# The first FFN product of the last two row groups as seven block products over eight PSUM banks

## The chip, the core and the metric

The kernel runs on one core of one Trainium2 chip. The metric is the device time of one execution in microseconds (us); the time before is 584.73 us, the median of three runs (584.64 to 585.35). The engines are named as in the profile: PE (TensorE, with PEld for its weight loads), DVE (VectorE), ACT (ScalarE), POOL (GpSimd) and SP (SyncE, which issues DMAs).

## What is computed

Attention with a squared ReLU, then a block of Fourier mixing, normalization and a feed-forward network (FFN):

```python
scores = (1 / sqrt(64)) * q @ k.T                      # 8 batches, 12 heads, 448 rows, 64 columns
x = (maximum(scores, 0) ** 2 / 448) @ v                # heads side by side: 8 x 448 x 768
u = x + real(fft(fft(x, axis=1), axis=2))
un = (u - mean(u)) / sqrt(var(u) + 1e-6)               # over the 768 columns
out = u + maximum(un @ w_ch1, 0) @ w_ch2               # w_ch1 768 x 3072, w_ch2 3072 x 768
```

The change touches `maximum(un @ w_ch1, 0)` for the last 512 of the 3584 rows.

## The kernel before

**Stages.** Batch after batch goes through attention (scores on PE, ReLU on ACT, square on DVE or ACT, product with v on PE), the mixing by DFT matrices, and the normalization; the normalized rows go to DRAM and come back transposed. The FFN runs over groups of rows: one of 384, one of 512, one of 384 and nine of 256 (`GT`, line 194; groups 0 to 11). Its matmuls fill PE between the parts of attention; after the last attention product only FFN groups are left.

**What sets the order.** All instructions are issued in an order that a planner in the kernel makes at build time (`Streams`, line 63). Every piece of work is a generator that asks with `need(engine, duration, deps, buffers)`; the planner takes the request that can start first by its own cost figures (`mm`, `act`, `dve`, line 141 on, and `LATENCY`, line 60). On the chip each engine runs its instructions in that order and waits on semaphores.

**PSUM.** There are eight banks: three tiles of two banks (`BS`, line 220, tags S0 to S2) and two single banks (`BF`, line 221). The FFN uses `BF`, attention and mixing mostly `BS`.

**A group's first product** (`ffn`, line 1383). `w1_sb[m][hf]` holds w_ch1 as six row blocks m of 128 and two column halves hf. For a group of 256 rows, `unT` holds the transposed rows as six blocks of 128x256. For each of 24 column blocks j, six matmuls (line 1452) sum up in half a bank; two blocks j share a bank, and `relu` (line 1409) moves 128x512 out to `h`, on ACT (line 1426) or DVE (line 1424). `unT` has two homes for the groups of 256 rows (`pair_homes`, line 1158), so the transposes of a group (line 1160) wait until the group two before has done its first product.

**A group's second product** (`Pair`, line 1536) is already done by seven block products (Strassen's scheme in Winograd's form), in two chains. Each product is 12 matmuls of 128x384 (line 1583). `chain_a` (line 1610) puts four products into one bank and `chain_b` (line 1631) one into one bank and two into another; after each, DVE adds the bank to an output tile `o` (line 1438), and the next product of that bank waits for this add (`t`). `early` and `late` (lines 1551 and 1572) form sums of blocks of `h` on DVE. The sums T of w_ch2 are made once (`weight_sums`, line 1281).

**Output tiles.** `outputs` (line 1353) has one stream for each of six slots: it loads a tile of u into `o` (line 1370), waits for the last add, stores it (line 1374), and waits for the store before it loads the next. Each group of 256 rows has four such tiles.

Of the kernel before, what the change touches and what calls it, by code (L numbers as in the profile page):

```python
# [9 lines left out]
FP32 = mybir.dt.float32  # L10
# [154 lines left out]
def kernel(  # L165
# [488 lines left out]
        BX[m].free.append(e)  # L654
        x_ready[b][m].t = e

    chains = [0]

    def attention(b, left=None):

# [8 lines left out]
        while pa < NB:  # L669
# [38 lines left out]
            for part in ("scores", "values") if few else ("values", "scores"):  # L708
                if part == "values" and values:
                    held = homes.take()  # L710
                    av = held[:, 0] if homes is BS else held
                    give = lambda when, homes=homes, held=held: homes.give(held, when)
                    vn, h0 = loads[bv * NG + mv // 2][2], 2 * mv % HG
                    for c in range(4):
                        sq, _, at = sv.pop(4 * mv + c)
                        sq_ids.append((e, at))
                        for h in range(2):
                            nc.tensor.matmul(av[h * Dh:(h + 1) * Dh, 0:S], lhsT=vn[:, c, h0 + h, :],  # L718
                                             rhs=sq[:, h, :], start=(c == 0), stop=(c == 3))
                        BSQ.free.append(e)  # L720
                    av_end = e - (n * mm(S) + SWITCH if n and not few else 0.0) + LATENCY["PE"]
                    if mv % 2 == 1:
                        BQ[2].free.append(e)
                    if left is None:
# [651 lines left out]
            yield need("SP", 0.0, [e])  # L1376

    def ffns():
        for b in range(NGR):
            yield need("SP", 0.0, [group_ready[b]])  # L1380
            yield from ffn(b)

    def ffn(b):
        T0, N, unT = groups[b]
# [24 lines left out]
        def relu(ph, e, j):  # L1409
# [18 lines left out]
            for x in ht[j:j + JN]:  # L1428
                x.t = e + LATENCY["ACT"]

        left = {(c, hf): 1 + (b > 0 and hf == 1 if c in WHOLES[b] else (c % 2, hf) != (0, 1))
                for c in range(NC) for hf in range(2)}

        def add(pc, e, c, hf, give=True):

            e = yield need("DVE", dve(DH), [e + LATENCY["PE"], ot[b, c, hf]])
            o = os[b, c, hf]
            nc.vector.tensor_tensor(o, pc[:, 0:DH], o, op=ALU.add)  # L1438
            if give:
                BF.give(pc, e)  # L1440
            left[c, hf] -= 1
            if not left[c, hf]:
                added[b, c, hf].t = e + LATENCY["DVE"]
            return e + LATENCY["DVE"]

        for j in range(0, JC, JN):
            hf, jj = divmod(j, JC // 2)
            e = yield need("PE", 6 * JN * mm(N), [w1_ready[hf]] + ([group_ready[b]] if b > 1 else []), [BF])
            ph = BF.take()
            for i in range(JN):  # L1450
                for m in range(MC):
                    nc.tensor.matmul(ph[:, i * N:(i + 1) * N], lhsT=w1_sb[m][hf][:, (jj + i) * 128:(jj + i + 1) * 128],  # L1452
                                     rhs=unT[:, m, 0:N], start=(m == 0), stop=(m == MC - 1))
            advance(6 * JN * mm(N))
            sch.add(relu(ph, e, j), (0, 0))
            if j == JC // 2:
                ffn_begun[b].t = e
                pairs = [Pair(b, c, h, ht, add, advance) for c in PAIRS[b]]
                for p in pairs:
                    sch.add(p.early(), (0, 0.3))  # L1460
                    sch.add(p.late(), (0, 0.3))
        if b == 0:
            unt_left.t = e
        else:
            BUNT.free.extend([e, e] if b == 2 else [e])

        for c in WHOLES[b]:
            if b > 0:
# [67 lines left out]
    class Pair:  # L1536
# [1 line left out]

        read = []

        def __init__(self, b, c, h, ht, add, advance):
            self.b, self.c, self.h, self.ht, self.add, self.advance = b, c, h, ht, add, advance
            self.L, self.R = slice(c * 128, c * 128 + 128), slice(c * 128 + 128, c * 128 + 256)
            self.ev = [slice(2 * i0, 2 * i1, 2) for i0, i1 in CH]
            self.od = [slice(2 * i0 + 1, 2 * i1, 2) for i0, i1 in CH]
            self.r12, self.r4 = ([Cell() for _ in CH] for _ in range(2))
            self.m1, self.m2, self.done = Cell(), Cell(), [Cell(), Cell()]
            self.reads = Cell(), Cell()
            self.waits, Pair.read = Pair.read, [self.reads[0], self.reads[1], *self.r4]

        def early(self):

            h, L, R_ = self.h, self.L, self.R
            if not made:
                yield need("DVE", 0.0, [un_left])
                a1 = work.tile([128, 6, 128], BF16, name="s1", tag="un2", bufs=1)
                a2 = work.tile([128, 6, 128], BF16, name="s2", tag="un3", bufs=1)
                at = JC * 256 + KP * DH
                for a, m in ((a1, upper(at, 6, 128)), (a2, upper(at + 6 * 128, 6, 128))):
                    made.append([a, m[:, 0:4], m[:, 4:6]])  # L1560
            for k, (i0, i1) in enumerate(CH):
                ev, od, s1, s2 = self.ev[k], self.od[k], made[0][k], made[1][k]
                d = dve2((i1 - i0) * 128)
                yield need("DVE", d, self.ht[2 * i0:2 * i1] + self.waits + ([upper_free] if k else []))
                nc.vector.tensor_tensor(s1, h[:, ev, R_], h[:, od, R_], op=ALU.add)
                yield need("DVE", d)
                nc.vector.tensor_tensor(s2, s1, h[:, ev, L], op=ALU.subtract)
                e = yield need("DVE", d)
                nc.vector.tensor_tensor(h[:, ev, R_], h[:, ev, L], h[:, ev, R_], op=ALU.subtract)
                self.r12[k].t = e + LATENCY["DVE"]  # L1570

        def late(self):

            h, L = self.h, self.L
            for k, (i0, i1) in enumerate(CH):
                e = yield need("DVE", dve2((i1 - i0) * 128), [self.m2, self.r12[k]])
                nc.vector.tensor_tensor(h[:, self.od[k], L], h[:, self.od[k], L], made[1][k], op=ALU.subtract)
                self.r4[k].t = e + LATENCY["DVE"]

        def product(self, pc, lhs, rhs, start, i0=0, i1=KP):  # L1580

# [5 lines left out]
        def first(self, k):  # L1587

            cut = KP - 3
            yield need("PE", cut * mm(DH), self.ht[k:2 * cut:2] + [self.m1] * k, [BF])  # L1590
            pc = BF.take()
            chains[0] += 1
            self.product(pc, self.block(k, self.L), self.weights(k, 0), True, 0, cut)
            e = yield need("PE", (KP - cut) * mm(DH), self.ht[2 * cut + k::2])
            self.product(pc, self.block(k, self.L), self.weights(k, 0), True, cut)
            return pc, e

        def block(self, k, cols):

            return [self.h[:, 2 * i + k, cols] for i in range(KP)]  # L1600

        def formed(self, n):

            return [made[n][k][:, i - i0] for k, (i0, i1) in enumerate(CH) for i in range(i0, i1)]

        def weights(self, k, hf):

# [23 lines left out]
        def chain_b(self):  # L1631
# [5 lines left out]
            e = yield need("PE", d, [sums[3]] + self.r12, [BF])  # L1637
            pc = BF.take()
# [27 lines left out]
    with tc.manual_schedule():  # L1666
# [11 lines left out]
        sch.add(attentions(), (3, 3))  # L1678
        sch.add(warming(), (9, 9))
        sch.add(weight_sums(), (6, 6))  # L1680
        sch.add(halve(), (3, 3))
        sch.add(turns(), (1, 1))
        for slot in range(6):
# [33 lines left out]
```

## Time and profile before

| | us |
|---|---|
| median of three runs | 584.73 |
| the profiled execution | 584.67 |
| its span, first to last instruction | 582.8 |
| PE busy in the span | 572.9 |
| DVE busy | 406.4 |
| ACT busy | 335.0 |
| POOL busy | 133.7 |

Busy time is summed over all stages. The view of windows gives it for a stretch of the span, with the granted PE clock (1.00 is full). A row of the chain of work names when a step began, how long it lasted, and its engine, tile, line and count. A row of groups ends with the busy time, the mean in ns, and the idle time before the group with what ended it. In the timeline a row gives start and length of a run of like instructions; in square brackets stands the idle time before it and its releaser.

### The profile page before, as it was taken

How to read it: one execution, taken by the hardware profiler on the slowest of the kernel's cores; microseconds unless marked ns; L12 is line 12 of the kernel's file. 1: busy time of each engine (PE TensorE's matmuls, PEld its weight loads, DVE VectorE, ACT ScalarE, POOL GpSimd, SP SyncE). 2: the span in 40 equal slices, each digit the busy share in tenths (PEclk: the TensorE clock that was granted, in tenths of full speed). 3: DMA queues.
4: the chain of work that ended last, by engine and by line, in shares of the span. 5: the costliest groups of instructions: out<-in, count | busy, mean ns of one | idle time of the engine just before them, and what ended most of it. 6: DMA issues, size and time to landing. Idle time of an engine off the chain costs nothing.

```text
span 582.8 us, 11457 instructions
## 1 busy us (share of the span) xinstructions
PE 572.9 (98%) x4476; PEld 365.7 (63%) x4476; DVE 406.4 (70%) x927; ACT 335.0 (57%) x511; POOL 133.7 (23%) x188
## 2 busy tenths in 40 slices
PE   8999999999999999999999999999999999999997
PEld 7566556544455546556857667568577786868684
DVE  5978667986669988787787878987946852222222
ACT  5866873587745787676668748777654340304040
POOL 8534021411115313421333032303300230000000
PEclk9998999999999999999999999999999999999999
DMA  9999999776947997699579987993433353031201
GB/s 120 206 211 227 222 210 134 173 131 95 181 57 189 207 172 168 116 216 167 122 123 207 180 153 147 200 176 115 126 75 100 118 151 99 30 94 36 79 30 55
DMA packets 133493, 81.85 MB, mean 140 GB/s; under 512 B 77504, under 2 KB 128704, under 8 KB 133440
## 3 DMA queue, kind: packets, MB, share of 16 engines
q0 software_dynamic: 40320, 33.63, 38.2%
q1 hardware_dynamic: 93120, 47.50, 36.3%
q8 instruction: 35, 0.57, 0.4%
q14 instruction: 18, 0.15, 0.1%
HBM read 62.91 MB, written 26.25 MB: 153 GB/s over the span
## 4 chain that ended last, share of the span: by engine, by line
PE 88%; DVE 6%; ACT 4%; issue 1%; POOL 0%; DVEq 0%; ACTq 0%; POOLq 0%
PE psF L1452 37%; PE psF L1583 26%; PE psS L736 6%; PE psF L718 5%; PE psF L1503 3%; PE psF L1477 3%; PE psS L1212 2%; ACT sq L761 2%; DVE sq L776 2%; PE psS L718 1%; PE psS L823 1%; PE psS L1026 1%; PE psS L1187 1%; PE psF L505 0%; ACT un L1087 0%
## 5 line engine op out<-in xcount | busy, mean ns | idle before, releaser
L1452 PE MATMUL psF<-unT,w 128*128 128x256 bf16 (+2 forms) x1728 | 229.8, 291 | 1.2 <-ACT unT L999 0.9
L1452 PEld LDWEIGHTS <-w 128*128 128x128 bf16 x1728 | 165.9, 98 | 61.6 <-issue 11.5
L761 ACT ACTIVATE sq<-psS 112x896 bf16<-112x896 f32 x192 | 164.4, 918 | 38.4 <-PE psS L736 38.0
L1426 ACT ACTIVATE hT<-psF 128x512 bf16<-128x512 f32 (+3 forms) x169 | 87.9, 532 | 116.6 <-PE psF L1452 115.8
L776 DVE TENSOR_TENSOR sq<-sq 112x896 bf16<-112x896 bf16 x161 | 100.6, 638 | 16.6 <-ACT sq L761 15.6
L1583 PEld LDWEIGHTS <-hT 128*128 128x128 bf16 x792 | 76.0, 98 | 54.4 <-issue 5.8
L1438 DVE TENSOR_TENSOR o<-psF,o 128x384 f32<-128x384 f32 x92 | 50.9, 553 | 44.8 <-PE psF L1583 39.6
L1583 PE MATMUL psF<-w,hT 128*128 128x384 bf16 x462 | 81.7, 326 | 0.3 <-DVE hT L1424 0.2
L736 PE MATMUL psS<-qkT 64*128 64x448 bf16 (+1 forms) x384 | 51.6, 359 | 1.2 <-ACT qkT L510 0.4
L718 PE MATMUL psF<-sq,vn 112*64 112x448 bf16 x320 | 37.9, 358 | 0.3 <-DVE o L1438 0.3
L557 DVE TENSOR_SCALAR xT<-psF 128x224 bf16<-128x224 f32 x58 | 19.8, 383 | 26.3 <-PE psF L718 26.2
L376 POOL DMA_DIRECT2D vn<-in_v_dram x24 | 17.3, 720 | 76.0 <-PE psS L736 67.7
L1059 POOL TENSOR_TENSOR u<-tp,xn 112x385 f32<-112x385 f32 (+2 forms) x14 | 13.3, 953 | 93.1 <-DVE tp L1041 81.5
L1583 PE MATMUL psF<-wsum,hT 128*128 128x384 bf16 x198 | 34.6, 326 | 0.0
L736 PEld LDWEIGHTS <-qkT 64*128 64x128 bf16 (+1 forms) x384 | 15.9, 102 | 28.7 <-issue 21.2
L376 POOL DMA_DIRECT2D qn<-in_q_dram x21 | 15.5, 739 | 69.9 <-DVE qkr L469 49.6
L718 PEld LDWEIGHTS <-vn 112*64 112x64 bf16 x384 | 17.8, 109 | 21.4 <-issue 13.7
L773 ACT ACTIVATE sq<-sq 112x896 bf16<-112x896 bf16 x31 | 29.5, 956 | 0.5
L1068 DVE BATCH_NORM_STATS2 stats<-u 112x6 f32<-112x384 f32 (+2 forms) x56 | 28.4, 541 | 0.0
L1087 ACT ACTIVATE un<-u,nmr,rstd 112x768 bf16<-112x768 f32 (+2 forms) x22 | 22.4, 1025 | 7.3 <-DVE nmr L1074 5.0
L1477 PE MATMUL psF<-w,hT 128*128 128x384 bf16 x144 | 25.1, 326 | 0.0
L1503 PE MATMUL psF<-w,hT 128*128 128x384 bf16 x144 | 24.7, 326 | 0.0
(166 smaller groups left out, 612.6 us busy)
## 6 DMA issues: line engine op xcount, KB each, us to landing
out_dram<-o SPq DMA_DIRECT2D x56, 192.0 KB, 2.2
vn<-in_v_dram POOLq DMA_DIRECT2D x24, 224.0 KB, 5.9
qn<-in_q_dram POOLq DMA_DIRECT2D x21, 224.0 KB, 5.3
kn<-in_k_dram POOLq DMA_DIRECT2D x21, 224.0 KB, 5.5
w<-in_moe_w_ch_dram POOLq DMA_DIRECT2D x12, 384.0 KB, 14.5
w<-in_moe_w_ch_dram POOLq DMA_DIRECT2D x4, 1152.0 KB, 20.5
utop<-u SPq DMA_DIRECT2D x12, 336.0 KB, 3.1
o<-utop SPq DMA_DIRECT2D x16, 192.0 KB, 3.8
```

What stands on the lines that cost most here:

```text
L376: nc.gpsimd.dma_start(out=t, in_=src[b, hs].rearrange("h (p j) d -> p h (j d)", j=4))
L718: nc.tensor.matmul(av[h * Dh:(h + 1) * Dh, 0:S], lhsT=vn[:, c, h0 + h, :], rhs=sq[:, h, :], start=(c == 0), stop=(c == 3))
L736: nc.tensor.matmul(sc[:wide, h, 0:S].rearrange("k (c q) -> k c q", c=4), lhsT=flat[ps, k0:k0 + wide], rhs=qT[ps, m % 2], start=True, stop= ...
L761: nc.scalar.activation(r, sc[:R, :, 0:S], AF.Relu)
L773: nc.scalar.activation(r, r, AF.Square)
L776: nc.vector.tensor_tensor(r, r, r, op=ALU.mult)
L1426: nc.scalar.activation(hs, ps, AF.Relu)
L1438: nc.vector.tensor_tensor(o, pc[:, 0:DH], o, op=ALU.add)
L1452: nc.tensor.matmul(ph[:, i * N:(i + 1) * N], lhsT=w1_sb[m][hf][:, (jj + i) * 128:(jj + i + 1) * 128], rhs=unT[:, m, 0:N], start=(m == 0), ...
L1477: nc.tensor.matmul(pc[:, 0:DH], lhsT=block(j, c), rhs=w2(j, hf), start=(j == 0), stop=(j == JC - 1))
L1503: nc.tensor.matmul(pc[:, 0:DH], lhsT=block(2 * i + k, c), rhs=weights[i], start=(start and i == 0), stop=(i == KP - 1), skip_group_check=True)
L1583: nc.tensor.matmul(pc[:, 0:DH], lhsT=lhs[i], rhs=rhs[i], start=(start and i == 0), stop=(i == KP - 1), skip_group_check=True)
```

## The change

Groups 10 and 11 get their first product together, in `last_two`, once both are transposed. With w_ch1 cut by halves of its rows (lo: m = 0 to 2, hi: m = 3 to 5) and by even and odd column blocks j, and with b1, b2 the transposed rows of groups 10 and 11, a 2x2 by 2x2 block product arises. `quarter_sums` forms on DVE the weight sums S1 = odd lo + odd hi, S2 = S1 - even lo, S3 = even lo - odd lo (in the place of odd lo), S4 = even hi - S2, 24 instructions of 128x768, and T1 = b2 lo - b1 lo, T2 = b2 hi - T1, T3 = b2 hi - b2 lo, T4 = b1 hi - T2, four more. For each pair of column blocks i = 0 to 11 there are seven products of three matmuls of 128x256:

- bank p (`main`): **M** = even lo x b1 lo; then **U2** adds S2 x T2, **U1** adds S1 x T1, **V** adds S4 x b2 hi. After M, U2 and U1 ACT copies the bank into SBUF; after V ACT applies the ReLU: that is the even block of group 11.
- bank r (`second`): **M'** = even hi x b1 hi. DVE adds the copy of M, then clamps at zero: the even block of group 10.
- bank q (`third`): **Q** = S3 x T3; DVE adds the copy of U1 and clamps: the odd block of group 11. Then **Q'** adds odd hi x T4; DVE adds the copy of U2 and clamps: the odd block of group 10.

U2, U1 and V wait for the copy before them; Q' waits for DVE's reading of q. The banks come from `B8`: the three two-bank tiles of `BS` as six banks, and the two of `BF`. Four sets of three copy tiles (`BK`) are in use in turn. `SLACK` (0.4) is added to what the planner assumes from a product to a copy and from a copy to a product. The ReLU results of group 10 lie where `h` lay, those of group 11 in tiles taken from attention.

The second products of both groups (`Pair`) are unchanged in their arithmetic; they take banks from `B8`, group 11's sums lie in four of the S tiles, and its `early` and `late` go in five pieces (of at most six column blocks) that don't cross its tiles. All four chains are in the planner's hands at once.

```diff
     def ffns():
-        for b in range(NGR):
+        for b in range(NGR - 2):
             yield need("SP", 0.0, [group_ready[b]])
             yield from ffn(b)
+        yield from last_two()
...
+    def quarter_sums():
+
+        yield need("SP", 0.0, [last_values])
...
+                yield from form(1, m, hf, w1_part(1, m, hf), w1_part(1, m + 3, hf), ALU.add)
+                yield from form(2, m, hf, S_[1][m, hf], w1_part(0, m, hf), ALU.subtract)
+                yield from form(4, m, hf, w1_part(0, m + 3, hf), S_[2][m, hf], ALU.subtract)
...
+                yield from form(3, m, hf, w1_part(0, m, hf), w1_part(1, m, hf), ALU.subtract, [ffn1_left],
+                                w1_part(1, m, hf))
...
+            e = yield need("DVE", dve2(768), [group_ready[ga], group_ready[gb]])
+            Tk[n] = homes[n - 1]
+            nc.vector.tensor_tensor(Tk[n], x(), y(), op=ALU.subtract)
...
+        B8 = Banks(6, lambda i: tiles[i // 2][:, i % 2] if i < 6 else plain[i - 6])
...
+        def product(ps, n, k, i, rhs, start, stop):
+
+            hf, ii = divmod(i, 6)
+            for m in range(3):
+                lhs = w1_part(n, m + k, hf)[:, ii] if k is not None else S_[n][m, hf][:, ii]
+                nc.tensor.matmul(ps[:, 0:N], lhsT=lhs, rhs=rhs[:, m], start=(start and m == 0),
+                                 stop=(stop and m == 2), skip_group_check=True)
+
+        d, half_done, SLACK = 3 * mm(N), Cell(), 0.4
+
+        late = LATENCY["PE"] + SLACK
+
+        def copy(ps, dst, e):
+            e = yield need("ACT", act(N), [e + late])
+            nc.scalar.copy(dst, ps[:, 0:N])
+            return e + LATENCY["ACT"] + SLACK
+
+        def sum_out(q, u, t, dst, deps, done, hta):
+            e = yield need("DVE", dve(N), deps, [BH[t]] if hta is not None else [])
+            nc.vector.tensor_tensor(dst, q[:, 0:N], u, op=ALU.add)
+            done(e)
+            e = yield need("DVE", 0.2)
+            nc.vector.tensor_scalar(dst, dst, 0.0, None, op0=ALU.max)
+            return e + LATENCY["DVE"] + SLACK
+
+        def main(i):
+
+            m1, u4 = Cell(), Cell()
+            e = yield need("PE", d, [], [B8, BK])
+            p, bk = B8.take(), BK.take()
+            cs = bk.aps
+            product(p, 0, 0, i, b1[:, 0:3], True, False)
+            sch.add(second(i, m1, cs), (5 + 0.1 * i, 5 + 0.1 * i))
+            m1.t = e = yield from copy(p, cs[0], e)
+            e = yield need("PE", d, [e, QS[2], QT[2]])
+            product(p, 2, None, i, Tk[2], False, False)
+            e = yield from copy(p, cs[1], e)
+            e = yield need("PE", d, [e, QS[1], QT[1]])
+            product(p, 1, None, i, Tk[1], False, False)
...
+            u4.t = e = yield from copy(p, cs[2], e)
+            e = yield need("PE", d, [e, QS[4]])
+            product(p, 4, None, i, b2[:, 3:6], False, True)
+            e = yield need("ACT", act(N), [e + late])
+            nc.scalar.activation(at_b(0, i, i + 1, every)[:, 0], p[:, 0:N], AF.Relu)
+            B8.give(p, e)
...
+        for n, p in enumerate(pairs):
+            sch.add(p.early(), (0, 7 + n))
+            sch.add(p.late(), (0, 7 + n))
+            sch.add(p.chain_a(), (7 + 1 * n, 0))
+            sch.add(p.chain_b(), (6.9 + 1 * n, 0))
+        yield need("SP", 0.0, pairs[1].done)
```

More of the change, by code (lines that the diff above doesn't have):

```diff
@@ L1378, in ffns, with adder, add @@
     def ffns():
-        for b in range(NGR):
+        for b in range(NGR - 2):
             yield need("SP", 0.0, [group_ready[b]])
             yield from ffn(b)
+        yield from last_two()
+    def adder(b, NC, pool):
+        left = {(c, hf): 1 + (b > 0 and hf == 1 if c in WHOLES[b] else (c % 2, hf) != (0, 1))
+                for c in range(NC) for hf in range(2)}
+        def add(pc, e, c, hf, give=True):
+            e = yield need("DVE", dve(DH), [e + LATENCY["PE"], ot[b, c, hf]])
+            o = os[b, c, hf]
+            nc.vector.tensor_tensor(o, pc[:, 0:DH], o, op=ALU.add)
+            if give:
+                pool.give(pc, e)
+            left[c, hf] -= 1
+            if not left[c, hf]:
+                added[b, c, hf].t = e + LATENCY["DVE"]
+            return e + LATENCY["DVE"]
+        return add
@@ L1429, in relu @@
                 x.t = e + LATENCY["ACT"]
[L1431 to L1444, printed above, removed]
+        add = adder(b, NC, BF)
         for j in range(0, JC, JN):
@@ L1457, in ffn @@
                 ffn_begun[b].t = e
-                pairs = [Pair(b, c, h, ht, add, advance) for c in PAIRS[b]]
+                at = lambda k, i0, i1, cols: h[:, 2 * i0 + k:2 * i1:2, cols]
+                pairs = [Pair(b, c, at, ht, add, advance, [(k, *ch) for k, ch in enumerate(CH)], BF) for c in PAIRS[b]]
                 for p in pairs:
@@ L1568, in early @@
                 e = yield need("DVE", d)
-                nc.vector.tensor_tensor(h[:, ev, R_], h[:, ev, L], h[:, ev, R_], op=ALU.subtract)
-                self.r12[k].t = e + LATENCY["DVE"]
+                nc.vector.tensor_tensor(at(0, i0, i1, R_), at(0, i0, i1, L), at(0, i0, i1, R_), op=ALU.subtract)
+                self.r12[x].t = e + LATENCY["DVE"]
         def late(self):
[L1574 to L1578, printed above, removed]
+            at, L = self.at, self.L
@@ new lines, in late, with sums @@
+            for x, (k, i0, i1) in enumerate(self.pieces):
+                e = yield need("DVE", dve2((i1 - i0) * 128), [self.m2, self.r12[x]])
+                nc.vector.tensor_tensor(at(1, i0, i1, L), at(1, i0, i1, L),
+                                        self.sums(1, i0, i1), op=ALU.subtract)
+                self.r4[x].t = e + LATENCY["DVE"]
+        def sums(self, n, i0, i1):
+            k = [c0 <= i0 < c1 for c0, c1 in CH].index(True)
+            return made[n][k][:, i0 - CH[k][0]:i1 - CH[k][0]]
@@ L1636, in chain_b @@
             yield from self.add(pc, e, c, 0)
-            e = yield need("PE", d, [sums[3]] + self.r12, [BF])
-            pc = BF.take()
+            e = yield need("PE", d, [sums[3]] + self.r12, [self.pool])
+            pc = self.pool.take()
             self.product(pc, self.block(0, self.R), T[3], True)
```

161 lines of the change are left out of this document (144 added, 17 removed).

## The prediction

> **What bounds the kernel now.** I read the page's parts 1 and 4 first, then the chain of work in order of time, then the windows of the last groups.
>
> ```profile
> span 582.8 us, 11457 instructions
> PE 88%; DVE 6%; ACT 4%; issue 1%; POOL 0%; DVEq 0%; ACTq 0%; POOLq 0%
> ...
> 491.19 15.72 PE psF L1452 x144
> 506.91 13.65 PE psF L1583 x84
> 520.56 15.72 PE psF L1452 x144
> 536.28 13.65 PE psF L1583 x84
> 549.93 15.72 PE psF L1452 x144
> 565.65 13.66 PE psF L1583 x84
> ...
> core 0: us, PE busy (x) PEld busy (x) DVE busy (x) ACT busy (x) POOL busy (x), PEclk, DMA share, GB/s
> 461.00:491.00 30.00, 30.00 (x234) 22.70 (x232) 16.05 (x39) 9.61 (x17) 4.59 (x5) 1.00 0.40 121
> 491.20:520.50 29.30, 29.30 (x229) 22.24 (x228) 8.45 (x19) 7.17 (x12) 0.00 (x0) 1.00 0.22 67
> 520.50:549.90 29.40, 29.40 (x231) 22.33 (x229) 8.46 (x19) 7.17 (x12) 0.00 (x0) 1.00 0.16 55
> ```
>
> The chain is TensorE (PE) without a gap from 491 us on: each group of 256 rows is 144 matmuls of 256 columns in 15.72 us (109.2 ns each) and 84 of 384 columns in 13.65 us (162.5 ns each). VectorE (DVE) works 8.46 us of the 29.4 and ScalarE (ACT) 7.17. So here a matmul left out is 109 ns of the end, as long as whatever it adds stays beside PE.
>
> **The change part by part.** The built order of the changed kernel has the same PE instructions as before up to the end of group 9 (520.56 us on the old clock); all that differs on PE is the last two groups.
>
> 1. *Removed.* 288 matmuls of the first product become 12 x 7 x 3 = 252; the 168 of the second product stay. 36 x 109.2 ns = **-3.93 us**.
>
> 2. *Added ahead of the stage, on DVE:* 24 sums of weight quarters and four of group columns, each bf16 of 128x768.
>
> ```profile
> L1565 DVE TENSOR_TENSOR s<-hT 128x768 bf16<-128x768 bf16 x11 | 6.0, 548 | 25.2 <-ACT hT L1426 25.2
> ...
> 506.94 1.18 SPq L1160 DMA_TRANSPOSE unT<-ntop  x1
> 508.16 1.42 SPq L1160 DMA_TRANSPOSE unT<-nbot  x1
> ...
> DMA to landing us min/median/max: 2.3/2.9/3.5
> ```
>
> 28 x 0.548 = 15.3 us. The windows leave DVE 14 us idle between 461 and 491 and 21 us up to 520.5, and the sums start after the last attention product. A sum that happens to stand ahead of an output add delays it by 0.55; the product waiting for that add comes one product (1.95 us) later, while the add's way is some 0.8 us (below), so 1.1 us are spare. I cost them at nothing; without that cover it is up to 0.55 for each such meeting. The four column sums need group 11's transposes, which can start only when group 9 has left its buffer (506.94). They land about 508.16 + 3.5 = 511.7 at the latest by the row (513.1 if counted from the end of the issue), and the sums stand behind group 9's third add, some 6 us after 506.9. Hidden, narrowly.
>
> 3. *Added in the stage.* Per block i, PE runs M, M', U2, U1, V, Q, Q' (three matmuls each: a slot of 0.328 us, 2.29 us a block), ACT four moves of 128x256, DVE three adds and three clamps of 128x256.
>
> ```profile
> L1426 ACT ACTIVATE hT<-psF 128x256 bf16<-128x256 f32 x18 | 6.9, 385 | 5.4 <-PE psF L1452 5.1
> L1438 DVE TENSOR_TENSOR o<-psF,o 128x384 f32<-128x384 f32 x92 | 50.9, 553 | 44.8 <-PE psF L1583 39.6 <-PE psF L1503 3.2 <-PE psF L1477 1.3
> L1424 DVE TENSOR_SCALAR hT<-psF 128x384 bf16<-128x384 f32 x9 | 5.0, 551 | 1.2 <-PE psF L1452 1.2
> L1424 DVE TENSOR_SCALAR hT<-psF 128x256 bf16<-128x256 f32 x6 | 2.5, 420 | 1.2 <-PE psF L1452 1.2
> ...
> 215.83 0.62 DVE L1424 TENSOR_SCALAR hT<-psF 128x256 bf16<-128x256 f32 x2
> 216.37 0.95 DVE L626 TENSOR_TENSOR fold<-folds 128x684 bf16<-128x684 bf16 x2
> ...
> 13.81 0.27 DVE L333 TENSOR_SCALAR channeg<-chan 128x386 bf16<-128x386 bf16 x1 [0.38 <-ACT chan L310]
> ```
>
> ACT: 4 x 0.385 = 1.54 of 2.29. The DVE add of 256 columns is not in the trace. At 384 columns the add takes 0.553 and a TENSOR_SCALAR out of PSUM 0.551; at 256 the latter takes 0.420, so I take 0.42 for the add (ends 0.27, at which two of 128x256 follow each other from 215.83 to 216.37, and 0.55). The clamp (bf16, in place) has its upper end at 0.27 (the 386 columns at 13.81) and can't be below nothing; I take 0.22. So DVE: 3 x 0.64 = 1.92 of 2.29, less what successive instructions overlap. Neither engine is the bound by rate; what counts is the way from a product back to PE.
>
> ```profile
> 520.40 3.88 PE L1452 MATMUL psF<-unT,w 128*128 128x256 bf16 x34
> 521.96 0.60 ACT L1426 ACTIVATE hT<-psF 128x512 bf16<-128x512 f32 x1 [14.35 <-PE psF L1452]
> ...
> 565.75 0.60 ACT L1426 ACTIVATE hT<-psF 128x512 bf16<-128x512 f32 x1 [0.72 <-PE psF L1452]
> 566.38 0.29 DVE L1565 TENSOR_TENSOR hT<-hT 128x256 bf16<-128x256 bf16 x1 [1.40 <-ACT hT L1426]
> ...
> 66.09 0.62 DVE L510 COPY qkT<-psF 128x896 bf16<-128x896 bf16 x1
> 66.77 0.39 PE L505 MATMUL psF<-ident,qn 112*64 112x112 bf16 x8 [0.23 <-DVE qkT L510]
> ...
> 577.19 2.11 PE L1583 MATMUL psF<-w,hT 128*128 128x384 bf16 x12
> 579.34 0.56 DVE L1438 TENSOR_TENSOR o<-psF,o 128x384 f32<-128x384 f32 x1 [1.39 <-PE psF L1583]
> ```
>
> PE to ACT: 12 matmuls from 520.40 are issued by 521.71, ACT starts at 521.96: 0.25. PE to DVE: 577.19 + 12 x 0.1625 = 579.14, then 579.34: 0.20. ACT to DVE: 566.35 to 566.38: 0.03. DVE to PE: 66.71 to 66.77: 0.06.
>
> In the built program the waits are stricter than the arithmetic. Two banks share one PSUM tile, so U2 of a block in such a tile waits not for its copy alone but for the DVE add that reads the neighbour bank; and PE signals M and M' together, after M'. The way is then 0.25 + 0.385 + 0.03 + 0.42 + 0.06 = **1.15 us** from the end of M' to U2. The order puts four slots there (M' of blocks 0, 1, 2 in slots 2, 4, 6; U2 in 7, 9, 11): 1.31 us, 0.16 spare. Where only three slots stand between, 0.98, PE waits about 0.17: V of block 2 behind Q of block 2 (slots 19 to 23) is the one in the first eight blocks. In the last four blocks four half-column sums in a row (0.55 each) stand in DVE's queue ahead of the add that V of block 9 needs: some 0.16 more. Counted along the built order by the same ways, 19 products in all have under 0.35 spare; the others should cost hundredths each. Sum **+0.35 us**; ends: 0 (all ways as short as their four slots) and, if each way is 0.3 longer, 19 x 0.25 = 4.7.
>
> 4. *The end.* Both groups' second products now run as one queue. Group 10's go first in pairs of chains; group 11's follow as third product of b, second of a, fourth of b, third of a, and then the fourth of a, with nothing left to put between the last two. The last product must wait for the add that empties its bank: 0.20 + 0.553 + 0.06 = **+0.81 us**. Before, two chains alternate to the end, so that each add has a whole product's time, and no row shows such a wait. Ends: 0.75 to 0.9.
>
> 5. *Moved.* Group 11's output tiles are reloaded into the slots of group 10.
>
> ```profile
> out_dram<-o SPq DMA_DIRECT2D x56, 192.0 KB, 2.2
> o<-utop SPq DMA_DIRECT2D x16, 192.0 KB, 3.8
> ```
>
> Store 2.2 + load 3.8 + hops = 6.3 us after group 10's add. The first such tile is needed by PE six products, some 11 us, later, the last one 10.6 us later (four products, the wait, one product). DVE stands still behind the first until it lands, with group 10's last adds queued after it; 4 us are spare. Hidden. After the last add all is as before: store and finish.
>
> Sum: -3.93 + 0.35 + 0.81 = -2.77. The profiled execution took 584.67 (span 582.8 and 1.87 around it), the median of the three runs is 584.73. **584.67 - 2.77 = 581.9 us.**
>
> **The rivals.**
>
> *The way is longer than its slots (slower).* With a way of 1.60 instead of 1.15, the 19 edge places wait 0.29 each, 5.5 us: 584.67 - 3.93 + 0.81 + 5.5 = 587.1. It decides from 1.47 on (3.1 us over 19 places). For it: the order is fixed, and PE can't pass a waiting product. Against: each hop above is a row. 5%.
>
> *DVE becomes the bound (no change).* If its instructions don't overlap, the stage with the second products that overlap it (some 32.6 us) holds 36 pairs of add and clamp (0.69 with the gap between dependent ones), 21 half-column sums (8.0) and an output add, 33.4 us of DVE; a full queue passes its unevenness to PE, which I put at 2 us: 584.67 - 3.93 + 0.35 + 0.81 + 2 = 583.9. Against: the pitch of 0.27. 11%.
>
> *The clock drops (slower).*
>
> ```profile
> 14.60:29.10 14.50, 13.95 (x165) 8.13 (x166) 14.07 (x34) 12.97 (x18) 8.22 (x22) 1.00 1.25 206
> 43.70:58.30 14.60, 13.22 (x141) 9.05 (x139) 11.96 (x29) 9.12 (x18) 6.42 (x7) 0.88 1.25 226
> ```
>
> Where PE was idle 1.38 of 14.6 us the granted clock was 0.88; with 0.55 idle it stayed 1.00. At 0.88 over 32.6 us: 4.4 more, 586.3. The forecast idles 0.35. 3%. The Trainium skill ("TensorE: Matmul & The Clock Gate", section "A second HAM failure mode: psum-queue depth-cycling") says that cycling through banks with frequent micro-idles makes the clock oscillate. By that rule this change would lose; the rows bear it out only where PE idled far more.
>
> *Signals cost PE time (faster, by less).* PE signals 64 times in the two groups instead of 38. If each held PE for 0.03, 0.8 us more: 582.7.
>
> ```profile
> 569.39 1.14 PE L1583 MATMUL psF<-wsum,s 128*128 128x384 bf16 x6
> ```
>
> Against: within one product, where no signal falls before the last matmul, six more (12 in 2.11 at 577.19, six in 1.14 here) add 0.97, 0.162 each; over seven products with their signals it is 13.65/84 = 0.1625. 9%. The same page, "The cost: per-tile semaphore tail", adds about 26 ns for each increment; by it the sum would be 582.6, and the trace does not show it.
>
> **How the numbers follow.** Forecast 72%; the rivals 5, 11, 3 and 9. The low end is no wait in the stage and 0.75 at the end, with 0.3 for the wobble of a run: 581.2. The high end takes in signals and the DVE case, 583.9, leaving out the two slower rivals and what lies beside them. A measurement of this kernel can tell about 0.2%, 1.17 us, from no change: faster means under 583.5. So faster 0.81, same 0.11, slower 0.08.
>
> **What would show it.** Right: 252 matmuls with PE idle under 0.6 us from the stage's start to the first product of the second kind, and one idle of 0.8 us before the last 12 matmuls, released by an output add. PE end about 2.8 us earlier. Wrong: PE idles of 0.1 to 0.4 released by adds or copies all through (the way), DVE busy over 95% there (the bound), a granted clock under 1.00, or any idle between 441 and 520 us (the sums ahead).

## The result and the profile after

The changed kernel takes **582.22 us**, the median of six runs (581.09 to 582.86), beside 584.68 for the kernel before in six runs on the same chip: 2.46 us less, a ratio of 0.9956 with a 95% interval of 0.9941 to 0.9971. The forecast was 581.9 in a range of 581.2 to 583.9.

The profiled execution took 582.86 us, with a span of 581.1. From its page, the span and the busy times:

```profile
span 581.1 us, 11519 instructions
PE 567.8 (98%) x4435; PEld 361.1 (62%) x4440; DVE 439.5 (76%) x1029; ACT 338.1 (58%) x537; POOL 134.4 (23%) x188
```

PE is busy 5.1 us less than before, DVE 33 us more: products became sums. Of the 5.1 us, 3.93 are the 36 matmuls that went; the rest is spread between executions, since a second profile of the kernel before has 571.0 us where the first has 572.9. The timeline of PE follows from group 8's first product on (start, length, and in brackets the idle time ahead). One line's length includes the last matmul's way through the array, so waits are read here from starts: so many matmuls of 0.1092 or 0.1625 us after the line before, a line should begin.

```profile
462.52 15.88 PE L1673 MATMUL psF<-unT,w 128*128 128x256 bf16 x144
478.35 4.06 PE L1812 MATMUL psF<-w,hT 128*128 128x384 bf16 x24
...
521.37 2.13 PE L1515 MATMUL psS<-unT,w 128*128 128x256 bf16 x18
523.33 0.49 PE L1515 MATMUL psS<-chan,quarter 128*128 128x256 bf16 x3
...
524.64 0.82 PE L1515 MATMUL psS<-chan,quarter 128*128 128x256 bf16 x6
...
528.25 0.92 PE L1515 MATMUL psS<-unT,quarter 128*128 128x256 bf16 x6
529.00 0.49 PE L1515 MATMUL psF<-chan,w 128*128 128x256 bf16 x3
...
547.38 0.27 PE L1515 MATMUL psF<-chan,quarter 128*128 128x256 bf16 x1
547.81 0.27 PE L1515 MATMUL psS<-unT,quarter 128*128 128x256 bf16 x1 [0.16 <-DVE hB L1529]
...
572.69 2.11 PE L1812 MATMUL psS<-w,quarter 128*128 128x384 bf16 x12
575.46 2.11 PE L1812 MATMUL psS<-w,hB 128*128 128x384 bf16 x12 [0.65 <-DVE o L1395]
```

There are four waits, and each can be worked out from two lines. At 478.35 PE is 0.11 late (462.52 + 144 x 0.1092 = 478.24). At 529.00 it is 0.09 late: the six matmuls of the line before are two products, the second of them V of block 2, and the line takes 0.92 where six in a row take 0.82, so PE waited inside it, ahead of V. At 547.81, V of block 9, it is 0.32 late; at 575.46, the last product, 0.82 (572.69 + 12 x 0.1625 = 574.64). The stage begins at 521.37, where group 10 began at 520.40 before: 0.97 later, which the forecast doesn't have. Of this, 0.86 is there at the start of group 8 (461.66 before), and 0.11 is the wait at 478.35. The experiments turn first to this.

The waits in the stage were forecast from durations that the trace before did not have. Here they are, in the view of groups for 521 to 552.9 us (the mean in ns stands after the bar):

```profile
L1524 ACT COPY copies<-psS 128x256 f32<-128x256 f32 x30 | 10.7, 372 | 21.1 <-PE psS L1515 19.2 <-DVE hT L1529 1.2 <-DMA o<-ubot 0.6
L1529 DVE TENSOR_TENSOR hT<-psS,copies 128x256 bf16<-128x256 f32 x15 | 6.3, 422 | 1.4 <-ACT copies L1524 1.3 <-PE psS L1515 0.2
L1532 DVE TENSOR_SCALAR hT<-hT 128x256 bf16<-128x256 bf16 x23 | 5.2, 227 | 0.8
```

### The profile page after: what moved, and what is told of

Read it like the earlier page. It is cut to its first block, busy times and chain, and to the rows that moved or that the text cites. A ratio compares the mean times of both kernels' runs of the same rounds, so it can differ in the third digit from the quotient of the medians.

```text
span 581.1 us, 11519 instructions
## 1 busy us (share of the span) xinstructions
PE 567.8 (98%) x4435; PEld 361.1 (62%) x4440; DVE 439.5 (76%) x1029; ACT 338.1 (58%) x537; POOL 134.4 (23%) x188
## 4 chain that ended last, share of the span: by engine, by line
PE 86%; DVE 8%; ACT 4%; issue 1%; DMA 1%; POOL 0%; SPq 0%; DVEq 0%; ACTq 0%; POOLq 0%
PE psF L1673 31%; PE psF L1812 21%; PE psS L738 6%; PE psF L718 5%; PE psS L1812 4%; PE psF L1727 3%; PE psF L1701 3%; PE psS L1515 3%; PE psS L1214 2%; ACT sq L763 2%; DVE sq L778 2%; PE psS L718 1%; PE psF L1515 1%; DMA unT<-nbot 1%; PE psS L825 1%
## 5 line engine op out<-in xcount | busy, mean ns | idle before, releaser
L1673 PE MATMUL psF<-unT,w 128*128 128x256 bf16 (+2 forms) x1435 | 197.2, 294 | 2.6 <-ACT unT L1001 0.9
L1673 PEld LDWEIGHTS <-w 128*128 128x128 bf16 x1440 | 137.5, 98 | 59.2 <-issue 12.4
L1660 ACT ACTIVATE hT<-psF 128x512 bf16<-128x512 f32 (+3 forms) x147 | 74.7, 521 | 69.6 <-PE psF L1673 66.9
L1812 PEld LDWEIGHTS <-hT 128*128 128x128 bf16 x720 | 69.0, 98 | 49.7 <-issue 5.8
L1812 PE MATMUL psF<-w,hT 128*128 128x384 bf16 x378 | 67.1, 326 | 0.3 <-DVE hT L1658 0.2
L1395 DVE TENSOR_TENSOR o<-psF,o 128x384 f32<-128x384 f32 x80 | 44.2, 553 | 28.6 <-PE psF L1812 23.4
L1812 PE MATMUL psF<-wsum,hT 128*128 128x384 bf16 x162 | 28.5, 326 | 0.0
L1701 PE MATMUL psF<-w,hT 128*128 128x384 bf16 x144 | 25.1, 326 | 0.0
L1727 PE MATMUL psF<-w,hT 128*128 128x384 bf16 x144 | 24.7, 326 | 0.0
```

The costliest lines, as they stand in the source:

```text
L1660: nc.scalar.activation(hs, ps, AF.Relu)
L1701: nc.tensor.matmul(pc[:, 0:DH], lhsT=block(j, c), rhs=w2(j, hf), start=(j == 0), stop=(j == JC - 1))
L1727: nc.tensor.matmul(pc[:, 0:DH], lhsT=block(2 * i + k, c), rhs=weights[i], start=(start and i == 0), stop=(i == KP - 1), skip_group_check=True)
L1812: nc.tensor.matmul(pc[:, 0:DH], lhsT=lhs[i], rhs=rhs[i], start=(start and i == 0), stop=(i == KP - 1), skip_group_check=True)
```

## The experiments

Moments of the whole execution wobble, as the first two runs show, so each run is compared by two stretches as well: from the start of group 8's first product to the start of group 10's first product (before) or of the seven-product stage (changed), both called the stage below, and from there to the start of the last product of 12 matmuls. The first stretch holds two groups, 8 and 9. The expectations of two later runs speak of the product that begins it as group 9's; by the rows it is group 8's.

### The changed kernel and the kernel before, once more

No edit in either.

> The changed kernel once more, unchanged. In its first profile the stage of the seven products began at 521.37 us, where group 10 had begun at 520.40 before; the stage itself and the end then saved 2.70 us. Theory: the 0.97 us ahead of the stage is the spread of one execution, because the instructions of PE are the same up to there and the shift came in steps at 205, 267 and 337 us, long before the added sums; the stage then begins between 519.5 and 521.5 us in other executions, and the median is 2.5 to 2.8 us below the kernel before. Rival: the delay belongs to the changed program; the stage begins at 521.2 to 521.6 us again and the median is only 1.7 us below.

> The kernel before once more, for its profile: theory: group 10 begins 0.3 us or more away from 520.40 us, as the place of this moment wobbles from execution to execution. Rival: it begins within 0.15 us of 520.40, and the later start in the changed kernel is its own.

Measured: the changed kernel 581.68 us (median of 12) beside 584.24 for the kernel before (median of 23), ratio 0.9957 (0.9942 to 0.9973). The starts, of the changed kernel's second profile and then of the kernel before's:

```profile
521.99 2.13 PE L1515 MATMUL psS<-unT,w 128*128 128x256 bf16 x18
...
576.07 2.11 PE L1812 MATMUL psS<-w,hB 128*128 128x384 bf16 x12 [0.65 <-DVE o L1395]
```

```profile
460.49 15.88 PE L1452 MATMUL psF<-unT,w 128*128 128x256 bf16 x144
...
519.23 15.88 PE L1452 MATMUL psF<-unT,w 128*128 128x256 bf16 x144
...
576.02 2.11 PE L1583 MATMUL psF<-w,hT 128*128 128x384 bf16 x12
```

| | group 8 begins | stage begins | last product begins | first stretch | second stretch |
|---|---|---|---|---|---|
| before | 461.66 | 520.40 | 577.19 | 58.74 | 56.79 |
| before, again | 460.49 | 519.23 | 576.02 | 58.74 | 56.79 |
| changed | 462.52 | 521.37 | 575.46 | 58.85 | 54.09 |
| changed, again | 463.14 | 521.99 | 576.07 | 58.85 | 54.08 |

The second profile of the kernel before begins group 10 1.17 us earlier than its first. The place of the stage wobbles by more than a microsecond from profile to profile of one program, while the stretches repeat to 0.01. The later start came again in this second profile of the changed kernel, at 521.99, which lies outside the range of the theory and of the rival. These two profiles alone would fit a delay of the changed program; but the median is 2.56 us below, not 1.7, and in five later variants with the same instructions ahead of the stage it begins between 519.47 and 520.57. So 0.86 of the 0.97 us was the execution's own, and 0.11 the change's; what moves the start was not settled. What the change does is in the stretches: +0.11 and -2.70, in sum **-2.59 us**, and the medians of the two sets of runs, -2.46 and -2.56, agree.

### The end: chain a of group 11 first

```diff
-            sch.add(p.chain_a(), (7 + 1 * n, 0))
+            sch.add(p.chain_a(), (7 + 1 * n - 0.2 * n, 0))
```

> Chain a of group 11 gets the better rank, so that the two chains alternate to the end and the last product has a whole product between it and the add that it waits for. Theory (the end costs 0.81 us, as the last of the seven products finds its bank still being read by the add): the idle of 0.82 us before the last 12 matmuls is gone, no other idle takes its place, and the time is 0.8 us below the changed kernel, 3.3 us below the kernel before. Rival: the chain's end only moves, because the output tile's reload or the sums of the ReLU results are late next; a wait of some tenths appears one or two products earlier, and less than 0.4 us is gained.

Measured: 580.30 us (median of six, 579.23 to 581.01), ratio 0.9931 (0.9909 to 0.9952) to the kernel before. The end in PE's timeline:

```profile
519.95 2.13 PE L1515 MATMUL psS<-unT,w 128*128 128x256 bf16 x18
...
571.28 2.11 PE L1812 MATMUL psF<-hT,hB 128*128 128x384 bf16 x12
573.23 2.11 PE L1812 MATMUL psS<-w,hB 128*128 128x384 bf16 x12
```

The last product follows 1.95 us after the one before, which is 12 x 0.1625: no wait is left there, and its start is 53.28 us after that of the stage instead of 54.08. The theory holds to 0.01 us; of the 1.38 us by which the median lies under the changed kernel's on this chip, the trace accounts for 0.80, and the rest is within the runs' spread.

### The sums ahead of the stage left out

```diff
-            nc.vector.tensor_tensor(home, x, y, op=op)
             S_[n][m, hf] = home
...
-                lhs = w1_part(n, m + k, hf)[:, ii] if k is not None else S_[n][m, hf][:, ii]
+                lhs = w1_part(n, m + k, hf)[:, ii] if k is not None else w1_part(n % 2, m, hf)[:, ii]
```

> Leaves out the 24 sums of weight quarters on DVE (the products read plain weight blocks in their place, so the output is another); the four sums of group columns, the order of all else and the number of matmuls stay. Theory (the sums ahead are hidden): DVE has some 13 us less to do between 450 and 521 us, PE stays without a gap, and the time is within 0.3 us of the changed kernel. Rival: the sums delay output adds, and through them PE; the time is 0.5 to 1.0 us below the changed kernel and the stage begins that much earlier.

Measured: 582.02 us (median of 11), 0.34 above the changed kernel. By the time nothing is gained. The trace says more: the first stretch is 58.74 us as before the change, so the wait of 0.11 us is gone. The second is 54.39, 0.31 longer: in this variant one copy on ACT waits 0.38 us for a DVE add, as its timeline shows, where the changed kernel has no such wait, and V of block 9 comes 0.31 later.

```profile
541.98 0.37 ACT L1523 COPY copies<-psS 128x256 f32<-128x256 f32 x1 [0.38 <-DVE hT L1528]
```

The add itself waits 0.34 us for an earlier copy, which in the changed kernel it does not; why was not traced. It hides what the time could show of the sums' cost; the first stretch, which ends before it, shows it.

So the sums cost 0.11 us of the first stretch. Ahead of it they cost nothing, though the first of them are formed there (from 449.09 us on): from the start of 21 matmuls of an earlier second product (446.21 us; 445.35 before) to that of group 8's first product it is 16.31 us in both kernels. The view of windows shows how they fit (stretch, its length, then busy times of PE, PEld, DVE, ACT and POOL with their counts, then the clock). Before:

```profile
449.00:478.00 29.00, 29.00 (x239) 22.92 (x237) 20.17 (x46) 12.22 (x21) 7.58 (x8) 1.00 0.42 131
478.00:520.00 42.00, 42.00 (x308) 29.93 (x306) 13.59 (x31) 7.34 (x13) 0.00 (x0) 1.00 0.23 66
```

The changed kernel, with its stage in the last row:

```profile
449.00:478.00 29.00, 29.00 (x238) 22.96 (x237) 27.80 (x63) 12.61 (x22) 7.17 (x7) 1.00 0.42 129
478.00:520.00 42.00, 42.00 (x308) 29.94 (x307) 18.30 (x42) 8.06 (x14) 0.94 (x1) 1.00 0.26 71
521.40:552.90 31.50, 31.34 (x275) 26.70 (x274) 25.42 (x80) 16.52 (x48) 0.00 (x0) 1.00 0.16 47
```

With the sums left out:

```profile
449.00:478.00 29.00, 29.00 (x234) 22.57 (x232) 18.68 (x47) 13.24 (x23) 7.51 (x8) 1.00 0.40 127
```

DVE is busy 27.80 of 29 us there. The window of the prediction, 461 to 491, mixed the end of this full stretch with the emptier one behind it.

### The sums twice

```diff
-            nc.vector.tensor_tensor(home, x, y, op=op)
+            for _ in range(1 if home is y else 2):
+                nc.vector.tensor_tensor(home, x, y, op=op)
```

> The 18 sums S1, S2 and S4 of weight quarters each run twice, 9.9 us more for DVE ahead of the stage; the order is the same. Theory (the sums are hidden, with 8 us of idle DVE from 461 to 491 us and 16 more up to 520): within 0.3 us of the changed kernel, and PE has no gap between 450 and 520 us. Rival: an output add that stands behind two sums in a row comes 1.1 us late, which uses up what is spare; gaps of some tenths appear in PE there, 0.5 us or more in all.

As built, the condition never held, so the six S3 ran twice too (formed in its own place, S3 then is odd lo again, so the output is another): 24 more sums, 13.2 us, 18 of them among S1, S2 and S4.

Measured: 592.47 us (median of four), ratio 1.0125 (1.0093 to 1.0157): some 10 us lost, where 0.3 was expected; the first stretch is 67.70 us, 8.85 more. What PE waits for from 440 to 592 us (sum, times, longest):

```profile
PE psF L1674 <- ACT hT L1661: 5.0, 3, 3.3
PE psF L1813 <- ACT hT L1661: 1.9, 1, 1.9
PE psS L1028 <- DVE pc L1233: 1.4, 1, 1.4
PE psF L1813 <- DVE o L1395: 0.9, 2, 0.5
```

The releaser named most is a ReLU copy on ACT, not DVE. ACT's timeline shows why it is late:

```profile
478.71 0.29 ACT L1073 ACTIVATE std<-mv,eps_t 112x1 f32<-112x1 f32 x1 [4.45 <-DVE mv L1071]
478.91 1.06 ACT L1661 ACTIVATE hT<-psF 128x512 bf16<-128x512 f32 x2
480.51 1.03 ACT L1089 ACTIVATE un<-u,nmr,rstd 112x768 bf16<-112x768 f32 x1 [0.53 <-ACT hT L1661]
```

ACT stands 4.45 us before the square root of the last normalization but one, which needs DVE's statistics; these are queued behind the sums. Two ReLU copies stand behind it on ACT, and PE waits for the banks that they empty. In the changed kernel the same chain is only just tight. The last normalization (`un`) waits 0.37 us for DVE's `nmr`, and two ReLU copies come behind it; PE, which needs the bank that the first of them empties, goes on at 478.35, 0.11 us late:

```profile
476.79 1.03 ACT L1089 ACTIVATE un<-u,nmr,rstd 112x768 bf16<-112x768 f32 x1 [0.37 <-DVE nmr L1076]
477.72 1.31 ACT L1660 ACTIVATE hT<-psF 128x512 bf16<-128x512 f32 x2
```

The rival that the expectation named, late output adds, is there with 0.9 us at the doubled S3, in group 9's second product, but the main loss has another way, through ACT. Two runs test this.

### S1 twice, and S4 later

```diff
-            nc.vector.tensor_tensor(home, x, y, op=op)
+            for _ in range(2 if n == 1 else 1):
+                nc.vector.tensor_tensor(home, x, y, op=op)
```

> Only the six sums S1 run twice: 3.3 us more for DVE, all of it between 449 and 478 us. Theory (all 24 sums run twice cost 10.2 us, because the sums stand ahead of the last normalization in DVE's queue, the ReLU copies on ACT stand behind its instructions, and PE waits for its banks; DVE has 1.2 us left in 29): PE waits for ReLU copies of group 9 by 2 to 3 us more than in the changed kernel. Rival (the loss came from the doubled S3 or from the sheer amount, and a small amount still fits): under 0.5 us.

Measured: 584.74 us, the time of the kernel before (ratio 1.0014, 0.9993 to 1.0034). PE's timeline:

```profile
460.79 6.97 PE L1674 MATMUL psF<-unT,w 128*128 128x256 bf16 x60
467.91 4.09 PE L1674 MATMUL psF<-unT,w 128*128 128x256 bf16 x36 [0.15 <-ACT hT L1661]
473.64 5.40 PE L1674 MATMUL psF<-unT,w 128*128 128x256 bf16 x48 [1.64 <-ACT hT L1661]
479.78 4.06 PE L1813 MATMUL psF<-w,hT 128*128 128x384 bf16 x24 [0.74 <-ACT hT L1661]
```

By the starts PE waits 0.57, 1.80 and 0.90 us, all for ReLU copies; the first stretch is 62.00 us, 3.15 more, for 3.3 us of added sums, a little above the 2 to 3 of the theory and far from the rival. The cover has no spare: from here on an added microsecond of DVE is nearly a microsecond of the end.

The other run takes the end of the second experiment and forms S4 behind the wait for the last normalization:

```diff
-                yield from form(4, m, hf, w1_part(0, m + 3, hf), S_[2][m, hf], ALU.subtract)
...
         yield need("DVE", 0.0, [un_ready[B - 1][1]], [BXN] + [BQ[2]] * 3)
+        for hf in range(2):
+            for m in range(3):
+                yield from form(4, m, hf, w1_part(0, m + 3, hf), S_[2][m, hf], ALU.subtract)
```

> The better order of the end (chain a of group 11 first, as in the second experiment), and the six sums S4 are formed only after the last normalization instead of among S1 and S2; the order of PE is the same as in the second experiment. Theory (DVE is full from 449 to 478 us, and the changed kernel pays 0.11 us there, at the end of group 9's first product, while DVE is idle more than half of the time after 478 us): the 0.11 us ahead of group 9's second product is gone, no gap comes in its place, and from the start of group 9's first product to the last product of all PE takes 0.1 us less than in the second experiment; the median is 3.3 to 4 us below the kernel before. Rival: the 0.11 us belongs to something else in the changed order and stays, or the later sums delay output adds of group 9.

Measured: 581.20 us (median of 10, 579.96 to 583.18), ratio 0.9944 (0.9927 to 0.9962).

```profile
462.62 15.88 PE L1675 MATMUL psF<-unT,w 128*128 128x256 bf16 x144
478.34 4.06 PE L1814 MATMUL psF<-w,hT 128*128 128x384 bf16 x24
```

478.34 is 462.62 + 15.72: the wait is gone. DVE's busy time from 449 to 478 falls from 27.80 to 25.80 us, less than the 3.3 us of six sums. DVE's timeline shows why:

```profile
469.37 0.69 DVE L1660 TENSOR_SCALAR hT<-psF 128x512 bf16<-128x512 f32 x1 [0.20 <-PE psF L1675]
...
475.92 0.69 DVE L1660 TENSOR_SCALAR hT<-psF 128x512 bf16<-128x512 f32 x1
```

With DVE less full, the planner gave it two of group 8's twelve ReLU copies; in the changed kernel all twelve are ACT's. So two things changed, and which of them took the wait away this run can't say; that the sums caused it rests on the run without them, in which all twelve stay with ACT. From group 8's start to that of the last product it is 112.01 us (58.74 and 53.27), beside 112.12 in the second experiment and 112.94 in the changed kernel. What the theory said of PE holds in the trace; 0.11 us is too little to be seen in times that spread over 2 us. The medians of the two better versions, 580.30 and 581.20, don't tell which is faster; by the stretches both beat both kernels.

### Without the longer way

```diff
-        d, half_done, SLACK = 3 * mm(N), Cell(), 0.4
+        d, half_done, SLACK = 3 * mm(N), Cell(), 0.0
```

> SLACK = 0 instead of 0.4: the longer way is left out of the order and all else stays. Theory (what counts is how many slots the order puts between a product and the next one of its bank): counting along this order with the ways that the traces show (0.25 from PE to ACT, 0.37 for the copy, 0.42 for the add, 0.05 for a hop), some ten places of the stage wait between 0.06 and 0.5 us, 3.6 us of waits to the end of PE where the changed kernel has 1.2: 2.4 us slower than the changed kernel, about the time of the kernel before. Rival: the engines are quicker than the planner assumes and the longer way isn't needed; the time is within 0.5 us of the changed kernel.

Measured: 584.23 us, no different from the kernel before (ratio 0.9992, 0.9974 to 1.0009). The second stretch is 56.22 us, 2.14 more than the changed kernel's. What PE waits for most from 519 us on (sum, times, longest), by what the brackets of the timeline show (about 0.16 less each than the starts give):

```profile
PE psS L1515 <- ACT copies L1524: 0.6, 3, 0.2
PE psS L1515 <- DVE hT L1529: 0.5, 2, 0.3
PE psS L1515 <- ACT hB L1556: 0.4, 1, 0.4
```

By the starts nine lines are 0.29 to 0.55 us late, 3.37 us in all, where 3.6 was counted and the changed kernel has 1.23. Eight of the nine, 3.04 us, lie in the stage, where the changed kernel has 0.41; the ninth, 0.32, stands among the last products, where the changed kernel has 0.82. So the seven products alone would gain next to nothing; the order with the longer way is worth four fifths of the gain.

### A longer way in the same order

Copies in halves, and then in quarters:

```diff
-            nc.scalar.copy(dst, ps[:, 0:N])
+            for c in 0, 128:
+                nc.scalar.copy(dst[:, c:c + 128], ps[:, c:c + 128])
```

```diff
-            nc.scalar.copy(dst, ps[:, 0:N])
+            for c in range(0, 256, 64):
+                nc.scalar.copy(dst[:, c:c + 64], ps[:, c:c + 64])
```

> Each of the 36 copies of 128x256 goes as two of 128x128; the planner isn't told, so the order of PE is the same. The way from a product to the next one of its bank becomes some 0.18 us longer, 1.33 instead of 1.15, against four slots of 1.31. Theory: a wait moves all later products with it and gives them room, so that only five or six places wait, by 0.06 to 0.26 us each: 0.6 us slower than the changed kernel, and PE's time from the start of the stage to its last product is 54.7 instead of 54.08. Rival (the sum with which the prediction bounded this term from above): each of 19 places with under 0.35 us to spare waits by itself, 2 to 3 us slower.

> Each of the 36 copies of 128x256 goes as four of 128x64, in the same order of PE. In halves the two parts overlapped and took 0.43 us instead of 0.37, so that the way became only 0.06 longer and not 0.18. By the pitch of those halves (0.16 at 128 columns, less at 64) four parts take 0.55 to 0.65, and the way is some 0.2 us longer, 1.34, where four slots give 1.31. Theory: a wait gives all later products room; half a dozen places wait, and PE takes 54.5 to 54.9 us from the start of the stage to its last product, where the changed kernel takes 54.08. Rival: each of the 19 places with under 0.35 us to spare waits by itself, 0.1 us or more each; 56 us and more.

Halves: 582.60 us (ratio 0.9971, 0.9949 to 0.9993), second stretch 54.34, 0.26 more. ACT's timeline (the first pair) shows that two halves take 0.43 us, only 0.06 longer than one copy, so this run lengthened the way too little to tell the two views apart:

```profile
520.40 0.43 ACT L1525 COPY copies<-psS 128x128 f32<-128x128 f32 x2 [13.65 <-PE psS L1515]
```

Quarters: 584.21 us in a single run, second stretch **55.50**, 1.42 more. In 21 of the 36 copies the four parts take 0.56 us, 0.19 longer than one copy, as the second row shows; in the 15 others, which queue behind the copy ahead of them, 0.60 to 0.76:

```profile
523.57 0.66 ACT L1525 COPY copies<-psF 128x64 f32<-128x64 f32 x4
...
526.00 0.56 ACT L1525 COPY copies<-psS 128x64 f32<-128x64 f32 x4
```

Seven lines of the stage are 0.11 to 0.35 us late by the starts, 1.83 us in all, where the changed kernel has two with 0.41. So the way became 0.2 longer, as expected, only where copies don't queue, and 55.50 lies between the theory's 54.5 to 54.9 and the rival's 56: neither holds. The theory had the added time at 0.4 to 0.8 us, too little; the rival had all 19 places late, where seven are. The upper end that the prediction set to this term, 19 places of 0.25 or 4.7 us for a way 0.3 longer, no run reached. That a wait gives the later places room fits this, but wasn't tried by itself.

### Each clamp twice

```diff
             nc.vector.tensor_scalar(dst, dst, 0.0, None, op0=ALU.max)
+            nc.vector.tensor_scalar(dst, dst, 0.0, None, op0=ALU.max)
```

> Each of the 36 clamps at zero runs twice: 8.2 us more for DVE, which is busy 25.4 of the 31.5 us of the stage. The order is the same and nothing else changes. Theory (DVE is not the bound now, but near it): 33.6 us of work don't fit in 31.5 without the overlap of successive instructions; PE waits at a dozen places, and the time is about 4 us above the changed kernel. Rival: DVE has room, since successive instructions overlap by some 0.1 us each; under 1 us slower.

Measured: 586.95 us (ratio 1.0037, 1.0021 to 1.0054); second stretch 58.59, 4.50 us more than in the changed kernel, where 4 was expected. PE's longest waits (brackets again):

```profile
PE psS L1515 <- DVE hB L1529: 1.4, 2, 1.2
PE psS L1515 <- DVE hT L1529: 0.9, 2, 0.6
```

The window of its stage:

```profile
520.50:556.00 35.50, 32.57 (x273) 26.46 (x272) 30.95 (x110) 16.18 (x48) 0.00 (x0) 1.00 0.14 42
```

DVE is not the bound in the changed kernel, with 25.42 of 31.5 us, but 8.2 us more cost 4.50, most of it in waits for DVE, at a busy share of only 87%: an uneven queue passes its waits to PE well before DVE is full.

## Why the prediction was right

By its own steps, against the stretches, which don't wobble:

1. *36 matmuls less, -3.93 us.* Right. The stretch before is 288 x 0.10917 + 156 x 0.1625 = 56.79, as measured; with 252 it would be 52.86, and 54.09 is that and the waits.
2. *The sums ahead, nothing.* The cost is **0.11 us** and not nothing, and the reason failed: of the 14 us in which DVE is idle between 461 and 491, more than half (7.9) lie after 478, where none of S1, S2 and S4 is formed. From 449 to 478 DVE had 8.83 us left, and its busy time rose by 7.63 of them. The prediction priced a sum ahead of an output add; what comes late first is the last normalization, then the ReLU copies behind it on ACT, then PE's banks. Six more sums cost 3.15 us. The column sums were hidden, as said.
3. *Waits in the stage, +0.35.* Measured 0.09 + 0.32 = 0.41. Both places are those named, V of block 2 and V of block 9, but the sizes were to be 0.17 and 0.16: one wait is half of that, the other twice, and that the sum fits so well is luck. None of the other edge places costs anything visible. The copy took 0.372 (0.385 assumed), the add 0.42, the clamp 0.227 (0.22).
4. *The end, +0.81.* Measured 0.82 and, in the second profile, 0.81; taken away by the order of two chains, it is gone.
5. *Reloads hidden; the rest of the end as before.* Right: PE waits for no tile's load, and from the end of the last product to that of the span it is 3.69 us (581.1 - 577.41) beside 3.66 before (582.8 - 579.14).

Sum: -3.93 + 0.11 + 0.41 + 0.82 = **-2.59** where -2.77 was said. Of its signs, one misled: PE's end was to come 2.8 us earlier, and in the two profiled executions it came 1.73 earlier, since their stages began 0.97 us apart. One sign of being wrong did show, an idle between 441 and 520 us: the 0.11 of step 2.

Of the rivals, the way stayed within its slots. DVE was at 81% in the stage. The granted clock was 1.00 in the stage, and it stayed 1.00 in the run with clamps twice, where PE stood still 2.93 of 35.5 us at a dozen places. The Trainium skill ("TensorE: Matmul & The Clock Gate", section "A second HAM failure mode: psum-queue depth-cycling") would expect an oscillating clock of such micro-idles; no run here shows it. Signals cost nothing: the four products from 523.33 to 524.64, at least two of which ACT copies next, take 1.31 us, 12 x 0.1092. The same page of the Trainium skill, section "The cost: per-tile semaphore tail", has about 26 ns for each increment, there for matmuls that share the array as tiles; for the whole-array matmuls here the trace does not show it.

## What to carry to other kernels

Look for idle time of the covering engine in the stretch in which the added work must run, not in a window around it, and follow every queue behind it: a sum on DVE cost nothing until it delayed a statistic that ACT waited for, with PE's banks queued behind. Count slots between a product and the next one of its bank against the way through the other engines; an order that respects this way was worth four fifths of this gain, and the last product of a chain needs another chain beside it. When starts wobble by a microsecond, compare stretches between two events of the same trace.

## What was not expected of the hardware

Two copies of 128x128 that follow each other on ACT take 0.43 us, hardly longer than one of 128x256 (0.372), and four of 128x64 mostly 0.56: with no other copy ahead of the four, each part starts 0.10 to 0.13 us before the one before ends. The Trainium skill ("ScalarE: Activation LUTs", section "What ACT_TABLE_LOAD costs") gives some 93 ns for the overlap of ACTIVATEs; the copies here show a little more. With the order of PE the same, the start of the stage lay between 519.23 and 521.99 us in the profiles, while the 58.85 us ahead of it and the 54.08 us after it repeated to 0.01 us.
